# Regrouping the last weight loads of a decode block and spreading part of one projection's rows over 64 partitions

## The chip, the cores and the metric

The kernel runs on one core of a Trainium2 chip. The metric is the device time of one execution in microseconds (us). Before the change the median of three runs is 237.1 us (237.0 to 237.11).

## The reference, cut to what matters

One decode step of a transformer block with adaptive layer norm, for two sequences (B = 2), model width D = 512, all in float32:

```
mod = silu(c) @ w_mod                          # six vectors sa, ca, ga, sb, cb, gb of width 512
h   = layernorm(x) * (1 + ca) + sa
q   = h @ wq                                   # 512 x 4096: 32 heads of 128
p   = softmax(q . k / sqrt(128))               # last 4096 of 32768 cached keys, 8 key/value heads
x   = x + ga * ((p . v) @ wo)                  # 4096 x 512
h   = layernorm(x) * (1 + cb) + sb
x   = x + gb * (silu(h @ w1) @ w2)             # 512 x 1792 and 1792 x 512
```

Nearly all of the work is reading: 32 tiles of 2 MB of keys and values, 8 MB each of wq and wo, 6 MB of w_mod, and 3.5 MB each of w1 and w2; 97.5 MB in all.

## The kernel before, in words

**Loads.** All transfers are issued by SyncE (SP), in program order, and go into a ring of eight buffers of 16 KB a partition (`ring`, `RING = 8`, `stream` at line 69). A buffer is given out anew when the instructions that read its last content are done, so a load waits for the reader of the load eight places before it. Besides, eight semaphores go round among the transfers, so that a transfer also waits until the one eight transfers before it has landed; SP waits in order, and whatever is behind a waiting load waits with it. The order is w_mod (4 loads, line 103 and 111, with four small loads of c and x between them, line 107), wq (4 loads of 128 rows, line 112), then for each key/value head the keys and the values of both sequences (`fetch`, line 324), then wo (4 loads, line 472), a small one of x (`x_sp`, line 474), w1 (3 loads, line 477) and w2 (5 loads, line 482). With `out` these are 58 transfers.

**Modulation and q.** TensorE (PE) multiplies silu(c) by w_mod as each load lands. VectorE (DVE) makes the normed and modulated input and turns it into hq_T (line 263), 128 rows by four blocks. The q loop (lines 281 to 291) runs over four blocks of 128 rows of wq, two halves n of the heads and four groups g, with matmuls of 32 x 512 that accumulate over the blocks; for one n and g the 512 columns are those of four heads (s) that lie apart in wq.

**Attention.** For each of eight key/value heads DVE turns the keys (line 337), PE makes the scores (line 349), then come maxima, exponentials, a turn of the probabilities and the weighted sum of the values (line 423). The order is written out by hand (`keep_in_program_order`).

**wo, second norm, feed-forward.** PE multiplies by wo as its loads land (lines 548 to 570), DVE makes the residual and the norm, and the loop at line 593 multiplies by w1, block k by block k: blocks 0 and 1 lie in the first load, 2 and 3 in one each. After block 1 it makes the variance (line 606). Its result `hp` is turned, scaled, put through silu and stands as uT (line 627). The loop at 629 multiplies the first eight 128-row blocks of w2 (`WIDE = 8`) into yw, 32 x 512 each; the loop at 641 multiplies the last six into y, 32 x 128 each; after block 10, `gather` (line 519) adds yw, copied by ScalarE (ACT), into y. Two DVE instructions (lines 653 and 654) and the store (line 656) end the kernel.

**busy(n)** (line 534) issues n matmuls of 32 x 256 into a PSUM bank that nothing reads, to keep PE occupied between loads. One matmul of the source is two on the chip, each with its own weight load, since the data are float32.

Lines are those of the kernel before.

Of the kernel before, what the change touches and what calls it, by code (L numbers as in the profile page):

```python
# [13 lines left out]
P = 128  # L14
B, D = 2, 512
HQ, HKV, DH = 32, 8, 128
# [7 lines left out]
def adaln_block(  # L24
# [21 lines left out]
    nc = tc.nc  # L46
# [16 lines left out]
    def const(shape, name):  # L63
        return consts.tile(shape, F32, name=name)

    def bank(tag, name):
        return (psum1 if tag in "CO" else psum).tile([P, 512], F32, tag=tag, name=name)

    def stream(name):
        return ring.tile([P, 4096], F32, tag="st", name=name)  # L70

    def load_rows(name, w, k, width):
        t = stream(f"{name}{k}")[:, :width]
        nc.sync.dma_start(t, w[k * P : (k + 1) * P, :])
        return t
# [15 lines left out]
    def load_runs(name, w, per, lo, hi):  # L91

        e = w.shape[1]
        t = stream(f"{name}{lo}")[:, : (hi - lo) * e].rearrange("p (q e) -> p q e", e=e)
        nc.sync.dma_start(t, w.rearrange("(p q) e -> p q e", q=per)[:, lo:hi, :])
        return t
# [12 lines left out]
                src[b, :].rearrange("(k a c) -> a k c", k=4, a=4),  # L109
            )  # L110
    wm += [load_rows("wm", w_mod, k, 6 * D) for k in range(1, 4)]
    wqt = [load_rows("wq", wq, k, HQ * DH) for k in range(4)]


    ident = const([P, P], "ident")
# [125 lines left out]
    for k in range(4):  # L241
        ab = wm[k][:, : 2 * D].rearrange("p (s k a c) -> p a s k c", s=2, k=4, a=4)
        cd = wm[k][:, 2 * D :].rearrange("p (s g m) -> p g s m", s=4, g=4)
        for g in range(4):
            r = slice(32 * g, 32 * g + 32)
            nc.tensor.matmul(m_ch[r, :], scT[:, k, :], ab[:, g], start=(k == 0), stop=(k == 3))
        for g in range(4):
            r = slice(32 * g, 32 * g + 32)
# [13 lines left out]
    hq_T = const([P, 4, 32], "hq_T")  # L262
# [13 lines left out]
    nc.gpsimd.memset(uT, 0.0)  # L276

    q_ps = [bank("D", f"q{n}") for n in range(2)]  # L280
    for k in range(4):
        wv = wqt[k].rearrange("p (n s g m) -> p n g s m", n=2, s=4, g=G)
        for n in range(2):
            for g in range(G):
                nc.tensor.matmul(  # L285
                    q_ps[n][32 * g : 32 * g + 32, :],
                    hq_T[:, k, :],
                    wv[:, n, g],
                    start=(k == 0),
                    stop=(k == 3),  # L290
                )
    for n in range(2):
        qT = once.tile([P, D], F32, tag="wide", name=f"qT{n}").rearrange("p (s j r) -> p s j r", s=4, r=32)
        nc.vector.transpose(qT.rearrange("p s j r -> p (s j r)"), q_ps[n])  # L294
        for g in range(G):
            r = slice(32 * g, 32 * g + 32)
            eng = nc.gpsimd if g % 2 else nc.vector
            eng.tensor_copy(
                qg[n][r, :, :, :, g], qT[r, :, :, 0:32:16].rearrange("p s j b -> p s b j")
            )  # L300
        rp = bank("C", f"qr{n}")[:, :P]
        nc.tensor.matmul(
            rp, rep4, qg[n].rearrange("p s b j g -> p (s b j g)"), start=True, stop=True
        )
        for i in range(4):
            r = slice(32 * i, 32 * i + 32)
            cp = nc.scalar.copy if i % 2 else nc.vector.tensor_copy
            cp(
                qbd[n][r].rearrange("p s b j c -> p (s b j) c")[:, :, 4 * i : 4 * i + 4],
                rp[r, :].rearrange("p (m g) -> p m g", g=G),  # L310
            )
# [162 lines left out]
    nc.sync.dma_start(rows8(x_sp), x2.rearrange("b (g m) -> g b m", m=P))  # L474
    xT = turned(x_sp, "xT")
    w1t = []
    for lo, hi in ((0, 2), (2, 3), (3, 4)):
        wt = load_runs("w1_", w1, 4, lo, hi)
        w1t.extend(wt[:, k, :] for k in range(hi - lo))
    T2, WIDE = F // P, 8  # L480
    w2t = {}
    for lo, hi in ((0, 4), (4, WIDE), (WIDE, 11), (11, 13), (13, T2)):
        wt = load_runs("w2_", w2, T2, lo, hi)
        for tt in range(lo, hi):
            w2t[tt] = wt[:, tt - lo, :]
# [9 lines left out]
    for r in (0, 64):  # L495
# [4 lines left out]
            start=True,  # L500
            stop=True,
# [32 lines left out]
    def busy(n):  # L534

        for _ in range(n):
            inorder(nc.tensor.matmul(  # L537
                junk[0:32, :256],
                id4,
                selh.rearrange("p m y -> p (m y)")[:, :256],  # L540
                start=True,
                stop=True,
            ))
# [4 lines left out]
    for q in range(24):  # L548
        g = q % 4
# [4 lines left out]
            start=(q < 4),  # L554
            stop=(q >= 20),
# [3 lines left out]
    for q in range(24, 32):  # L559
        for g in range(4):  # L560
# [4 lines left out]
                start=(q == 24),  # L565
                stop=(q == 31),
# [26 lines left out]
    for k in range(4):  # L593
        for g in range(4):
            inorder(nc.tensor.matmul(
                hp[32 * g : 32 * g + 32, :],
                hT[:, k, :],
                w1t[k][:, g * FC : (g + 1) * FC],
                start=(k == 0),
                stop=(k == 3),  # L600
            ))
        if k == 2:
            busy(2)
        if k == 1:
            var = bank("B", "var_b")
            inorder(nc.tensor.matmul(var[:, :B], mean512, vs, start=True, stop=True))
            std = once.tile([P, B], F32, tag="stdb", name="std_b")
            nc.scalar.activation(std, var[:, :B], AF.Sqrt, bias=eps_t)
            rstd = once.tile([P, B], F32, tag="rstdb", name="rstd_b")
            nc.vector.reciprocal(rstd, std)  # L610
    busy(5)
    nc.vector.tensor_mul(ax, ao, ga)
    nc.vector.tensor_add(x1, x_sp, ax)
# [15 lines left out]
    for tt in range(WIDE):  # L629
        g = tt % 4  # L630
        inorder(nc.tensor.matmul(
            yw[32 * g : 32 * g + 32, :],
            uT[:, tt, :],
            w2t[tt],
            start=(tt < 4),
            stop=(tt >= WIDE - 4),
        ))
        if tt % 4 == 3:
            busy(1 + tt // 4)
    y = bank("D", "acc_y")[:, :P]  # L640
    for tt in range(WIDE, T2):
        for g in range(4):
# [4 lines left out]
                start=(tt == WIDE),  # L647
                stop=(tt == T2 - 1),
# [35 lines left out]
```

## Time and profile before

| what | value |
|---|---|
| median of three runs | 237.1 us |
| the profiled execution | 236.89 us |
| its span (first to last instruction) | 235.0 us |
| mean granted TensorE clock | 0.869 |
| busy: PE, PEld, DVE, ACT, POOL | 146.5, 45.9, 114.6, 25.4, 10.3 us |
| read from HBM | 97.53 MB, 415 GB/s over the span |
| packets on SP's queue | 7,592 |

The page's span is that of one profiled execution; the 1.9 us between it and that execution's time lie around it. The page cuts the span into 40 slices of 5.9 us and gives for each the busy share of an engine in tenths; its row DMA is the mean over the core's 16 DMA engines. The chain of waits follows the work that ended last back from the end: an entry "DMA wo" is time in which that chain waited for a transfer of wo to land. The timeline gives instructions in order of time, neighbours of one line merged, with the idle time before them and what ended it in brackets. The packed trace also holds a record of every DMA packet (start, duration, bytes, queue) and of every semaphore increment by which a DMA engine tells that its share of a transfer has landed. q1 is the queue of the kernel's transfers, q8 and q14 are named instruction queues by the profile.

### The profile page before, as it was taken

Reading aid. Unit: us, or ns where it says so; the run is one execution under the profiler, and the core shown is the slowest. Engines: PE = TensorE matmul, PEld = TensorE weight load, DVE = VectorE, ACT = ScalarE, POOL = GpSimd, SP = SyncE. Lnnn points to the kernel's source line nnn. Section 1 sums busy time; section 2 is a strip of 40 time slices with the busy share of each in tenths; the row PEclk is TensorE's granted clock in tenths of the full one; section 3 lists DMA queues with packets and bytes.
Section 4 is the critical chain, followed back from the end, with each engine's and each line's share of the span. In section 5 each row is a group of like instructions: output and inputs, shape, how many; then the busy total and the mean of one; then the engine's idle time right before and its main releaser. Section 6 shows DMA issues by size and latency. Waiting matters only on the chain.

```text
span 235.0 us, 2644 instructions
## 1 busy us (share of the span) xinstructions
PE 146.5 (62%) x1094; PEld 45.9 (20%) x1094; DVE 114.6 (49%) x176; ACT 25.4 (11%) x56; POOL 10.3 (4%) x30
## 2 busy tenths in 40 slices
PE   0086546367187577667549519626743967788993
PEld 0032101101011121121112102111211222335332
DVE  0634000793694792693892792595298050002130
ACT  2200000100300200200200200200020021003210
POOL 8600000100000000000000000000000000000000
PEclk9999975759869997999976967965985799999999
DMA  6999999999999999999999999999999999999991
GB/s 253 426 438 427 427 438 427 424 439 427 429 441 424 427 438 427 429 438 424 429 435 429 427 432 432 432 429 432 428 429 429 429 432 429 432 426 422 421 412 56
DMA packets 7603, 97.69 MB, mean 416 GB/s; under 512 B 920, under 2 KB 936, under 8 KB 1576
## 3 DMA queue, kind: packets, MB, share of 16 engines
q1 hardware_dynamic: 7592, 97.54, 97.5%
q8 instruction: 8, 0.13, 0.2%
q14 instruction: 3, 0.02, 0.0%
HBM read 97.53 MB, written 0.00 MB: 415 GB/s over the span
## 4 chain that ended last, share of the span: by engine, by line
DMA 64%; DVE 22%; PE 10%; ACT 2%; issue 1%; SPq 1%; DVEq 0%
DVE kT L337 16%; DMA wo<-in_A_wo_dram 14%; DMA k<-in_A_k_cache_dram 14%; DMA v<-in_A_v_cache_dram 13%; DMA wq<-in_A_wq_dram 13%; DMA w<-in_B_w_dram 7%; PE s L349 5%; DMA wm<-in_w_mod_dram 3%; DVE zp L395 2%; PE o L423 2%; PE q L285 1%; DVE xp L393 1%; ACT pr L381 1%; DVE mx L359 1%; ACT L381 1%
## 5 line engine op out<-in xcount | busy, mean ns | idle before, releaser
L337 DVE STREAM_TRANSPOSE kT<-k 128x1024 f32<-128x1024 f32 x64 | 73.7, 1210 | 1.6 <-DMA k<-in_A_k_cache_dram 1.6
L349 PE MATMUL s<-kT,qbd 128*32 128x512 f32 x256 | 44.5, 670 | 11.2 <-DVE kT L337 11.1
L423 PE MATMUL o<-v,ptb 128*32 128x512 f32 x256 | 38.5, 730 | 19.8 <-DMA v<-in_A_v_cache_dram 19.3
L359 DVE TENSOR_REDUCE mx<-s 128x1 f32<-128x512 f32 x8 | 5.5, 691 | 40.1 <-PE s L349 40.1
L349 PEld LDWEIGHTS s<-kT,qbd 128*32 128x32 f32 x256 | 11.1, 126 | 45.8 <-issue 24.1
L285 PE MATMUL q<-wq,hq_T 128*32 128x512 f32 x64 | 11.2, 836 | 10.1 <-DMA wq<-in_A_wq_dram 10.1
L423 PEld LDWEIGHTS o<-v,ptb 128*32 128x32 f32 x256 | 8.1, 124 | 35.8 <-issue 33.1
L402 PE MATMUL pT<-zp,id 128*32 128x256 f32 x64 | 5.6, 418 | 13.9 <-DVE zp L395 13.9
L379 ACT COPY bias<-bp 128x1 f32<-128x1 f32 x8 | 1.3, 159 | 111.9 <-PE bp L377 111.9
L537 PE MATMUL junk<-selh,id 128*32 128x256 f32 x46 | 11.3, 380 | 0.0
L294 DVE STREAM_TRANSPOSE qT<-q 128x512 f32<-128x512 f32 x2 | 1.4, 718 | 18.6 <-PE q L285 18.3
L395 DVE TENSOR_TENSOR zp<-xp,group 128x1024 f32<-128x1024 f32 x8 | 9.8, 1225 | 0.2
L393 DVE STREAM_TRANSPOSE xp<-pr 128x512 f32<-128x512 f32 x8 | 5.6, 701 | 4.4 <-ACT pr L381 4.4
L217 PE MATMUL mean_a<-mv_a,avg 128*128 128x1 f32 x2 | 0.6, 362 | 10.6 <-DVE mv_a L214 10.6
L361 PE MATMUL mT<-ident,mx 128*1 128x128 f32 x16 | 3.0, 270 | 6.4 <-DVE mx L359 6.4
L550 PE MATMUL acc_o<-wo,oTn 128*32 128x512 f32 x48 | 5.8, 598 | 1.9 <-DMA wo<-in_A_wo_dram 1.6
L537 PEld LDWEIGHTS junk<-selh,id 128*32 128x32 f32 x46 | 5.0, 110 | 6.7 <-issue 3.5
L438 PE MATMUL o_all<-ob,selh 128*64 128x128 f32 x64 | 5.7, 304 | 0.8 <-ACT ob L432 0.8
L270 DVE STREAM_TRANSPOSE xT<-x_sp 128x128 f32<-128x128 f32 x1 | 0.4, 403 | 11.8 <-DMA x_sp<-in_A_x_dram 11.8
L432 ACT COPY ob<-o 128x512 f32<-128x512 f32 x8 | 4.7, 585 | 10.3 <-PE o L423 10.3
L285 PEld LDWEIGHTS q<-wq,hq_T 128*32 128x32 f32 x64 | 2.1, 128 | 18.8 <-DMA wq<-in_A_wq_dram 12.5
L249 PE MATMUL m_sp<-wm,scT 128*32 128x512 f32 x32 | 5.7, 796 | 0.0
(132 smaller groups left out, 95.0 us busy)
## 6 DMA issues: line engine op xcount, KB each, us to landing
k<-in_A_k_cache_dram SPq DMA_DIRECT2D x16, 2048.0 KB, 30.2
v<-in_A_v_cache_dram SPq DMA_DIRECT2D x16, 2048.0 KB, 31.5
wq<-in_A_wq_dram SPq DMA_DIRECT2D x4, 2048.0 KB
wo<-in_A_wo_dram SPq DMA_DIRECT2D x4, 2048.0 KB, 32.3
wm<-in_w_mod_dram SPq DMA_DIRECT2D x4, 1536.0 KB, 10.2
w<-in_B_w_dram SPq DMA_DIRECT2D x2, 1024.0 KB, 23.2
w<-in_B_w_dram SPq DMA_DIRECT2D x1, 1792.0 KB
w<-in_B_w_dram SPq DMA_DIRECT2D x2, 896.0 KB
```

What stands on the lines that cost most here:

```text
L249: nc.tensor.matmul(m_sp[r, :], scT[:, k, :], cd[:, g], start=(k == 0), stop=(k == 3))
L285: nc.tensor.matmul(q_ps[n][32 * g : 32 * g + 32, :], hq_T[:, k, :], wv[:, n, g], start=(k == 0), stop=(k == 3),)
L337: inorder(nc.vector.transpose(kT[h, b][:, :, 8 * n4 : 8 * n4 + 8, :].rearrange("p j n k -> p n j k"), kt[h, b][:, n4 * 1024 : (n4 + 1) * 1 ...
L349: inorder(nc.tensor.matmul(s_ps[h][r : r + 32, :], qbd[h // 4][:, h % 4, b, j, :], kT[h, b][:, j, 16 * c : 16 * c + 16, :], start=(j == 0) ...
L359: inorder(nc.vector.tensor_reduce(mx, s_ps[h], axis=AX.X, op=ALU.max))
L393: inorder(nc.vector.transpose(xp, pr[h]))
L395: inorder(nc.vector.tensor_mul(zp, xp[:, None, :, 0:16].to_broadcast([P, 4, 16, 16]), group[:, :, None, None].to_broadcast([P, 4, 16, 16]),))
L402: inorder(nc.tensor.matmul(tp[32 * i : 32 * i + 32, :], id4, zp.rearrange("p a s x -> p (a s) x")[:, :, 4 * i : 4 * i + 4], start=True, st ...
L423: inorder(nc.tensor.matmul(o_ps[h][32 * c : 32 * c + 32, :], ptb[h % 2][:, 256 * b + 32 * w : 256 * b + 32 * w + 32], vt[h, b][:, 512 * w ...
L438: inorder(nc.tensor.matmul(o_all[r : r + 64, :], selh[:, m, HQ - G - G * h : 3 * HQ - G - G * h], o_sb[h][:, m * DH : (m + 1) * DH], start ...
L537: inorder(nc.tensor.matmul(junk[0:32, :256], id4, selh.rearrange("p m y -> p (m y)")[:, :256], start=True, stop=True,))
L550: inorder(nc.tensor.matmul(acc[32 * g : 32 * g + 32, :], oTn[:, q, :], wot[q // 8][:, q % 8, :], start=(q < 4), stop=(q >= 20),))
```

## The change

Three things are done.

1. wq's last 128 rows are loaded without the columns of the last three heads (3,712 of 4,096 columns). These three heads' columns of the 128 rows go into a buffer of their own, `wqx`, on partitions 0 to 63: partition p holds rows 2p and 2p + 1. That takes eight loads of eight partitions each, with a step of four partitions, two behind each of the four loads of wq. `wqx` takes a place in the ring, ahead of wq's first block.
2. So that PE can use them, hq_T's last block is multiplied by the even and by the odd columns of the identity, which gives `hx` (64 partitions by two by 32), and for the three groups in question the last block's matmul has 384 columns in place of 512, followed by two matmuls of 128 columns over 64 partitions.
3. w1 comes in two loads of two blocks in place of three, and w2's first eight blocks in one load in place of two. The `busy` calls move with it: 6 after the variance in place of 2 after block 2, and 2 after all of yw in place of 1 and 2 after each half. There are 64 transfers in place of 58.

```diff
-    wqt = [load_rows("wq", wq, k, HQ * DH) for k in range(4)]
+    WX = 3 * DH
+    WN = HQ * DH - WX
+    wqt, wqx = [], stream("wqx")[:, : 2 * WX].rearrange("p (j e) -> p j e", j=2)
+    rows2 = wq[3 * P :, WN:].rearrange("(p j) e -> p j e", j=2)
+    for k in range(4):
+        if k < 3:
+            wqt.append(load_rows("wq", wq, k, HQ * DH))
+        else:
+            wqt.append(stream("wq3"))
+            nc.sync.dma_start(wqt[3][:, :WN], wq[3 * P :, :WN])
+        for p0 in ((0, 1), (2, 3), (32, 33), (34, 35))[k]:
+            nc.sync.dma_start(wqx[p0 : p0 + 29 : 4], rows2[p0 : p0 + 29 : 4])
...
+    hx = const([P // 2, 2, 32], "hx")
+    hxp = bank("B", "hxp")[: P // 2, :64]
+    for j in range(2):
+        nc.tensor.matmul(
+            hxp[:, 32 * j : 32 * j + 32], ident[:, j:P:2], hq_T[:, 3, :], start=True, stop=True
+        )
+    nc.vector.tensor_copy(hx.rearrange("p j c -> p (j c)"), hxp)
...
             for g in range(G):
+                r = slice(32 * g, 32 * g + 32)
+                part = k == 3 and n == 1 and g > 0
+                s1 = 3 if part else 4
                 nc.tensor.matmul(
-                    q_ps[n][32 * g : 32 * g + 32, :],
+                    q_ps[n][r, : s1 * DH],
                     hq_T[:, k, :],
-                    wv[:, n, g],
+                    wv[:, n, g, :s1, :],
                     start=(k == 0),
                     stop=(k == 3),
+                    skip_group_check=True,
                 )
+                for j in range(2 if part else 0):
+                    nc.tensor.matmul(
+                        q_ps[n][r, 3 * DH :],
+                        hx[:, j, :],
+                        wqx[: P // 2, j, (g - 1) * DH : g * DH],
+                        start=False,
+                        stop=(j == 1),
+                        skip_group_check=True,
+                    )
...
-    for lo, hi in ((0, 2), (2, 3), (3, 4)):
+    for lo, hi in ((0, 2), (2, 4)):
         wt = load_runs("w1_", w1, 4, lo, hi)
...
-    for lo, hi in ((0, 4), (4, WIDE), (WIDE, 11), (11, 13), (13, T2)):
+    for lo, hi in ((0, WIDE), (WIDE, 11), (11, 13), (13, T2)):
         wt = load_runs("w2_", w2, T2, lo, hi)
...
-        if k == 2:
-            busy(2)
         if k == 1:
...
             nc.vector.reciprocal(rstd, std)
+            busy(6)
...
-        if tt % 4 == 3:
-            busy(1 + tt // 4)
+    busy(2)
```

## The prediction

> **What bounds the kernel now.** I read the page's slices first, then its DMA queues.
>
> ```profile
> PE   0086546367187577667549519626743967788993
> DVE  0634000793694792693892792595298050002130
> PEclk9999975759869997999976967965985799999999
> DMA  6999999999999999999999999999999999999991
> GB/s 253 426 438 427 427 438 427 424 439 427 429 441 424 427 438 427 429 438 424 429 435 429 427 432 432 432 429 432 428 429 429 429 432 429 432 426 422 421 412 56
> ...
> q1 hardware_dynamic: 7592, 97.54, 97.5%
> q8 instruction: 8, 0.13, 0.2%
> q14 instruction: 3, 0.02, 0.0%
> ```
>
> No compute engine is full; the 16 DMA engines are, from the second slice to the last but one. In the packet records 5,102 of the 5,128 packets of 16 KB took 611 ns, and on one engine the next starts about 4 ns before the last ends: 16 x 16,384 B / 607 ns = 432 GB/s, the figure of the GB/s row. So each DMA engine is a conveyor without gaps, and the time is that of the engine that ends last, plus what follows it. The chain of waits in order of time shows the end:
>
> ```profile
> 181.22 32.69 DMA wo<-in_A_wo_dram
> 213.91 0.02 issue
> 213.92 0.02 SPq L95
> 213.94 0.03 issue
> 213.97 16.51 DMA w<-in_B_w_dram
> 230.48 0.04 issue
> 230.53 1.10 PE acc_y L643 x24
> 231.63 0.02 issue
> 231.66 0.30 DVE yo L653
> 231.96 0.02 issue
> 231.98 0.29 DVE yo L654
> ```
>
> Two stretches of waiting for transfers and 1.7 us of compute: what moves the landings of w2 moves the end. The landing records (one semaphore increment per DMA engine and transfer) show that the engines do not end together. For the last transfer (w2 rows 13) they come 0, 0.25, 0.33, 0.37, 0.48 / 0.78, 0.87, 1.24 / 1.45, 1.66, 1.86, 1.89, 1.96, 1.99, 2.00, 2.05 us after 229.07. The reason is in the two instruction queues above. Up to 28 us every transfer's sixteen landings lie within 0.64 us; each of q8's eight 16 KB packets (31.6, 77.2, 105.7, 128.7, 164.3, 185.4, 207.8, 221.9 us) then sets one engine back by some 1.5 us, a different one each time, and q14's three 8 KB packets (47.2, 168.6, 214.5) set back one more each by some 0.7. Eight late engines, three half late, five undisturbed: the sixteen offsets.
>
> **Term 1, the engines' load.** (a) wq's last 128 rows lose 1,536 B each. 14,336 B took 535 ns and 16,384 B 611, so 1,536 B are worth 57 ns; 8 rows on every engine: -0.46 us. (b) The eight wqx loads move 8 partitions x 2 pieces of 1,536 B. No such piece is in the trace; between 128 B (13 ns) and 2,048 B (84 ns) it is 65 ns, started 61 ns apart, and a semaphore packet adds 6. One load is then 2 x 61 + 6 = 0.128 us on each engine it uses, eight are +1.02 us. (c) Merging w1's two quarters saves 8 x (2 x 268 - 531) ns = 0.04, w2's two fours 8 x (2 x 305 - 607) = 0.02, two semaphore packets 0.01: -0.08 in all. Engines without wqx get -0.53 us, the others +0.49.
>
> Everything hangs on which engines get wqx. No eight-row load is in the trace. The nearest rows: the loads of c and x (4 rows) land with 4 increments, on four engines; so does x_sp. x_sp lands at 212.20, 212.31, 212.39 and 213.26, right behind wo's last rows, whose sixteen landings run from 211.85 to 213.91 at offsets 0, 0.17, 0.28, 0.35, 0.37, 0.54, 0.55, 0.82, 1.22 and then seven from 1.48 up. Three of the four are among the earliest; the pattern 0, 0.11, 0.19, 1.06 fits 0.17, 0.28, 0.35 and 1.22. So the four engines of small loads are not among the late eight. I take it that an eight-row load uses these four and four more, and that these too are of the other half, since late and not late are exactly eight and eight; bounds: none late, or at least one.
>
> The Trainium skill speaks to this in "DMA: Bandwidth & Descriptors", section "Why a DMA increments its semaphore by 16 and not by 1": the number of engines is the largest up to 16 that divides both slowest dimensions, and they are the lowest-numbered. By it eight rows go to the lower half, which holds the four; the trace agrees for four rows, and nothing here tells whether the late eight are the upper half.
>
> With none late, the merged w2 rows 0 to 7 take the place of w2 rows 4 to 7, whose last landings were at 1.26 (half late) and 2.06 (late) behind 225.33: 1.26 + 0.49 = 1.75, 2.06 - 0.53 = 1.53. The last is now 1.75: **-0.31 us**. For the last transfer it is the same (1.24 and 2.05). With one late engine hit it is +0.49.
>
> **Term 2, the tail's compute.** These PE rows of the timeline carry it:
>
> ```profile
> 225.98 1.06 PE L631 MATMUL acc_yw<-w,uT 128*32 128x512 f32 x8 [0.36 <-DVE uT L627]
> 227.43 1.06 PE L631 MATMUL acc_yw<-w,uT 128*32 128x512 f32 x8
> 228.32 1.03 PE L537 MATMUL junk<-selh,id 128*32 128x256 f32 x4
> 229.36 0.86 PE L643 MATMUL acc_y<-w,uT 128*32 128x128 f32 x24
> 230.01 0.43 PE L524 MATMUL acc_y<-acc_y_sb,id 128*32 128x128 f32 x8
> 230.53 1.06 PE L643 MATMUL acc_y<-w,uT 128*32 128x128 f32 x24
> ```
>
> Before, half of yw was done ahead of the landing at 227.39, since w2 rows 0 to 3 were there. Now all 16 matmuls start with that landing. Eight took 0.88 us to the next start (227.43 to 228.32), 16 take 0.86 more: junk starts at 229.18. Its four at 0.216 end at 230.04 (before, acc_y waited until 229.36 for w2 rows 8 to 10). Then 24 of acc_y (0.65 to the next start): 230.69; gather: 230.91; 16 of acc_y: 231.35; the last eight, which before began at 231.16, with the landing at 231.12. 0.19 later by an unmoved landing; the last eight then run in a stream (0.109 apart, where after the wait they were 0.133 apart), so the end is **+0.15 us** later, which I take. The yw copy on ACT (0.59) ends near 230.05, ahead of the gather.
>
> What stands before yw has cover. w1 rows 2 and 3 come together at 222.48. busy(6) after var (220.33) runs 12 x 0.216 = 2.6 us, to 222.93, so hid's second half starts 0.41 later than its last quarter did, and lasts two quarters (1.5 in place of 0.75): hidT comes 1.16 us later and uT lets yw start at 227.14. That hides behind the landing at 227.39 with 0.25 to spare; all these times move together with the landings. Were the cover gone, what it lacks would be paid in full. The matmuls fed to PE leave no gap longer than about 0.8 us, so I leave the clock as the PEclk row has it (9 in the last eight slices).
>
> **What costs nothing.** hx: two matmuls and one DVE copy, done when hq_T is ready, ahead of wq's first landing (22.9 us). q: three matmuls of 384 columns in place of 512 and six of 128, below 0.6 us before the first keys at 45.95; SP's k and v issues run some 30 us ahead of the landing (30.2 and 31.5 us on the page), so half a microsecond there is invisible. SP: eight more issues of 0.45 to 0.72 us. wqx takes a ring buffer, so the fourth k load waits for the last q matmul (42.4 us, now about 43) and five loads queue behind it; the engines then still hold k loads that land until 53.5. Ten us of cover. At the end w2's loads wait for older buffers than before and are issued earlier.
>
> **Sum.** -0.31 + 0.15 = -0.16 us. The profiled execution took 236.89 (span 235.0 and 1.9 around it), so it would be 236.73; the median of the runs is 237.1, so I predict **236.9**. A measurement of this kernel tells about 0.2% (0.47 us) from no change.
>
> **Rivals.** (A) At least one late engine is among wqx's eight. For it: two thirds of the engines that small loads were not seen on are late. Landing +0.49, tail +0.15: 237.7, slower. It decides as soon as an engine with an offset over 1.57 (1.57 + 0.49 = 2.06) gets wqx rows. 0.14. (B) The half-late engine is not hit (q14's packet falls elsewhere), or the tail costs nothing: last landing 1.53, -0.53 and 0 to 0.15: 236.6 to 236.7. 0.12. (C) PE fetches a ninth time. q8's packets started when 204, 464, 748, 962, 1,262, 1,448, 1,747 and 2,021 PE instructions had begun, 260 apart; the next would be near 2,281 of now some 2,266 (2,219, 11 matmuls of 4, 3 waits). If it comes, it comes beside w2's last packets and sets an engine back 1.5 us: 1.52 + 1.5 = 3.0 against 2.05, so 238.0. 0.06. (D) A small load holds its engines longer than its bytes. Upper bound: SP's 0.57 us an issue, 8 x 0.57 = 4.6 in place of 1.02, last landing 1.26 + 4.0 = 5.3: 240.4; by the 0.18 us between the landings of c's and x's loads 1.44: 2.17, so 237.4. Against both: the packet records of those loads are gapless on their four engines. 0.03.
>
> Here the Trainium skill speaks against the change: "DMA: Bandwidth & Descriptors", section "Rules for kernel authors", says that under 64 KB one pays mostly overhead, and its section "Anatomy of one DMA" gives about 2.0 us a transfer (by GpSimd's path). A wqx load has 24 KB; eight would add 16 us if the engines stood still meanwhile, and by the packet records they do not.
>
> My forecast (no change beyond 0.2%) has 0.65. Faster by over 0.2%: 0.12 (0.09 of B, 0.03 of the forecast's spread). Slower by over 0.2%: 0.22 (A, C, 0.01 each of D and of that spread). Within: 0.66. Range 236.5 (B, less the runs' spread of 0.1) to 237.8 (A with the same).
>
> **What would show it.** Right: the landings of each transfer after wq spread over about 1.5 to 1.75 us in place of 2.05, the last w2 landing near 230.8, yw as one block of 16 that starts with a landing, and the last acc_y not waiting for a DMA. Wrong: a landing spread of 2.5 (A), a ninth q8 packet (C), idle time in the packet records around 20 to 45 us (D or SP), or yw waiting for uT.

## The result, and the profile after

| | before | after |
|---|---|---|
| median of the runs | 237.1 us (5 runs, 237.0 to 237.29) | 237.92 us (5 runs, 237.76 to 238.26) |
| the profiled execution, its span | 236.89, 235.0 us | 237.84, 235.9 us |
| first and last landing of w2 rows 13 | 229.07, 231.12 us | 229.16, 231.94 us |
| PE instructions in the records | 2,219 | 2,266 |

The ratio is 1.0034 (95% interval 1.0022 to 1.0045, written in brackets below): slower by 0.34%, 0.8 us. The forecast was 236.9 and "no change"; its range ended at 237.8. Of the runs further down, e11 stands by its four executions of 238.23 to 238.65 us alone: the fifth, which is its profiled one, fell into a slower state (251.22 us), so e11 has no trace to read.

The page of the kernel after, the same rows as before:

```profile
PE   0087275738718775775758529627744967878984
DVE  0634001288279298396595793594298050002130
PEclk9999978875967999999979976995995799999999
DMA  6999999999999999999999999999999999999991
GB/s 248 420 428 433 411 421 437 419 435 436 419 436 431 431 428 433 436 419 439 428 431 428 431 433 428 432 431 431 433 425 433 425 436 428 425 441 425 425 398 39
...
q1 hardware_dynamic: 7496, 97.54, 97.2%
q8 instruction: 9, 0.15, 0.2%
q14 instruction: 3, 0.02, 0.0%
```

DMA is still 9 from the second slice on. What differs is GB/s in slices five and six (23.6 to 35.4 us): 411 and 421 where before had 427 and 438. The engines are busy there and move less: that is where the wqx loads run. The ninth q8 packet of rival C came, at 232.7 us, when all loads had landed.

The end of the chain of waits of the kernel after, in order of time:

```profile
196.97 31.31 DMA w<-in_B_w_dram
228.28 0.14 issue
228.41 1.92 PE acc_yw L665 x16
230.34 0.52 PE junk L572 x3
...
232.03 0.72 PE acc_y L676 x19
232.77 0.30 DVE yo L686
233.09 0.29 DVE yo L687
```

No wait for a transfer stands in the chain after 228.41; before it stood ahead of the last 24 matmuls of acc_y. The whole end hangs on the landing of w2 rows 0 to 7 at 228.28. That landing is 0.89 us later than the one that yw's second half waited for before (227.39), and the first DVE instruction of yo starts 1.11 later (231.66, now 232.77). So 0.89 is landings, 0.22 is the tail. Of the 0.89, 0.12 is there already at w_mod's third load (mean landing 14.06 and 14.18 us).

The timeline of the kernel after shows that nothing else holds yw:

```profile
227.79 0.20 DVE L661 TENSOR_TENSOR uT<-z,sgh 128x28 f32<-128x28 f32 x1
228.41 1.92 PE L665 MATMUL acc_yw<-w,uT 128*32 128x512 f32 x16 [0.71 <-DMA w<-in_B_w_dram]
```

uT is done at 227.99, 0.29 ahead of the landing; the bracket names the DMA.

The late landings go back to one place. The rows of the stretches from 26 to 32 us, from the tables by stage of before and after (us; busy time and number for PE, PEld, DVE, ACT, POOL; granted clock; DMA share; GB/s):

```profile
26.00:32.00 6.00, 3.19 (x16) 0.52 (x16) 0.00 (x0) 0.00 (x0) 0.00 (x0) 0.72 1.02 434
```

```profile
26.00:32.00 6.00, 2.65 (x16) 0.60 (x16) 0.00 (x0) 0.00 (x0) 0.00 (x0) 0.78 1.00 404
```

404 in place of 434 GB/s over 6 us is 0.18 MB not moved, 0.4 us of all sixteen engines. The packet records say how. Of the 128 pieces of 1,536 B, 107 took 62 to 65 ns. The other 21 lie in the first two pairs of loads: three of them at 22.2 to 22.5 us, and 18 at 27.3 to 28.1, up to 342 ns. 33 of the 16 KB packets between 20 and 32 us took 622 to 798 ns, where 611 is the rule. (One more took 1,102 ns at 27.8; it follows q8's first packet, 26.8 to 27.7 us, as one of 1,115 ns at 32.5 follows q8's first packet in the kernel before, so it is not counted here.) All pieces of the third and fourth pair (32.7 to 38.2 us) took 62 to 65 ns. I call those that took longer than usual **dear packets**.

### The profile page after: what moved, and what is told of

It is laid out like the page before. It is cut to its first block, busy times and chain, and to the rows that moved or that the text cites. A ratio compares the mean times of both kernels' runs of the same rounds, so it can differ in the third digit from the quotient of the medians.

```text
span 235.9 us, 2697 instructions
## 1 busy us (share of the span) xinstructions
PE 151.4 (64%) x1116; PEld 48.4 (21%) x1116; DVE 115.0 (49%) x177; ACT 25.4 (11%) x56; POOL 10.3 (4%) x30
## 4 chain that ended last, share of the span: by engine, by line
DMA 57%; DVE 20%; PE 18%; ACT 2%; issue 1%; SPq 0%; DVEq 0%
DMA v<-in_A_v_cache_dram 28%; DVE kT L372 14%; DMA w<-in_B_w_dram 13%; DMA wq<-in_A_wq_dram 13%; PE s L384 7%; PE o L458 4%; DMA wm<-in_w_mod_dram 3%; DVE zp L430 2%; PE q L310 2%; ACT pr L416 1%; DVE xp L428 1%; DVE mx L394 1%; PE q L319 1%; PE acc_yw L665 1%; PE mT L396 1%
## 5 line engine op out<-in xcount | busy, mean ns | idle before, releaser
L384 PE MATMUL s<-kT,qbd 128*32 128x512 f32 x256 | 45.9, 659 | 11.2 <-DVE kT L372 11.2
L310 PE MATMUL q<-wq,hq_T 128*32 128x512 f32 (+1 forms) x64 | 12.1, 730 | 8.4 <-DMA wq<-in_A_wq_dram 8.4
L572 PE MATMUL junk<-selh,id 128*32 128x256 f32 x52 | 12.4, 380 | 0.0
L572 PEld LDWEIGHTS junk<-selh,id 128*32 128x32 f32 x52 | 5.6, 110 | 6.4 <-issue 2.4
L412 PE MATMUL bp<-negscale,mrow 1*128 1x1 f32 x16 | 3.0, 256 | 4.2 <-DVE mrow L405 4.2
```

The lines of the kernel that those rows point to most:

```text
L310: nc.tensor.matmul(q_ps[n][r, : s1 * DH], hq_T[:, k, :], wv[:, n, g, :s1, :], start=(k == 0), stop=(k == 3), skip_group_check=True,)
L384: inorder(nc.tensor.matmul(s_ps[h][r : r + 32, :], qbd[h // 4][:, h % 4, b, j, :], kT[h, b][:, j, 16 * c : 16 * c + 16, :], start=(j == 0) ...
L572: inorder(nc.tensor.matmul(junk[0:32, :256], id4, selh.rearrange("p m y -> p (m y)")[:, :256], start=True, stop=True,))
```

## The experiments

Each run is compared with the kernel before on the same chip. e1 to e4, e11 and e14 to e16 are forms of the change. e5 to e7, e9 and e10 are the kernel before with extra loads that nothing reads, in a place of the ring; e8 and e12 add three tiny loads; e13 (e15 in eight loads) gave no result. The theories at the start: it is the engines' bytes (rival A), the tail, or the price of the small loads.

**e1: the third part alone** (w1, w2 and `busy` as in the change, wq as before).

> The change without its wq part: w1 in two loads, w2's first eight rows in one, the busy calls moved; 56 transfers. Theory (the eight small wqx loads put bytes on DMA engines that are late already): the landings come 0.08 us earlier and the end of PE's last block 0.15 to 0.22 later, so +0.07 to +0.15 us against the kernel before, 237.2 us. Rival (the regrouped tail costs the time): +0.6 to +0.9, 237.8.

237.01 against 237.06, ratio 0.9999 [0.9991, 1.0008]. Its chain of waits ends like that of the change:

```profile
195.53 32.31 DMA w<-in_B_w_dram
227.98 1.92 PE acc_yw L630 x16
...
231.59 0.72 PE acc_y L641 x19
232.34 0.30 DVE yo L651
```

The same form of tail, and no loss: the merged transfers give back (last landing 0.10 us earlier by the account below) what the tail adds.

**e2: the first two parts alone** (wqx and hx; w1, w2 and `busy` as before).

> The change's wq part alone, with the loads of w1 and w2 and the busy calls of before; 66 transfers. Theory: the last landing is that of an engine that gets wqx rows and an instruction packet, 0.5 us later from its bytes and 0.3 more from the stall around 26 to 30 us, +0.7 to +0.9 us: 237.9. Rival (the tail costs the time): +0 to +0.2, 237.2. Second rival (bytes alone, the stall being chance): +0.5, 237.6.

237.97, ratio 1.0042 [1.0029, 1.0055]. The whole loss is in wq's part.

**e3: the change with wqx spread over sixteen engines.**

```
-        for p0 in ((0, 1), (2, 3), (32, 33), (34, 35))[k]:
-            nc.sync.dma_start(wqx[p0 : p0 + 29 : 4], rows2[p0 : p0 + 29 : 4])
+        nc.sync.dma_start(wqx[k : 64 : 4], rows2[k : 64 : 4])
```

> The change with wqx in four loads of 16 partitions in place of eight loads of 8: the same pieces of 1,536 bytes, the same matmuls, but each of the 16 DMA engines takes 8 of them in place of eight engines taking 16. Theory (which engines get the bytes decides): each engine gets 4 x 0.128 - 0.46 - 0.08 us, about nothing, so what remains is the tail: 237.2 to 237.3, landings spread over 2.05 us behind the first. Rival (small pieces cost time wherever they go: the stall of 0.3 us): 237.5 to 237.6.

239.06 (238.06 to 240.14), ratio 1.0088 [1.0063, 1.0113]. A miss: without any unevenness of bytes it is slower still. In its records most 16 KB packets from 36 to 50 us take 690 to 704 ns; why is open. With this loss of its own the run can't tell what uneven bytes cost; e5 to e9 do.

**e4: the change with one head in place of three** (`WX = DH`, so pieces of 512 B).

> The change with one head's columns in wqx in place of three: pieces of 512 bytes, still eight loads of eight partitions. By the packet times (27 ns for 512 bytes) the engines with wqx get 8 x 0.052 - 0.15 - 0.08 = +0.19 us in place of +0.49, the others -0.23. Theory: the last landing is 0.3 us earlier than with three heads, 237.6 if the stall stays, 237.3 without it. Rival (cost per load, not per byte): as with three heads, 237.9.

237.09, ratio 1.0002 [0.9993, 1.001]: no loss at all, better than expected. All 128 pieces took 27 ns.

**e5, e6, e7: the kernel before with eight extra loads of 1,536 B pieces.** e5 reads one dense stretch of w2, e6 the rows that the change reads (16 KB between the pieces of a partition, 128 KB between engines), e7 is e5 with four partitions a load.

```
+    rows2 = wq[3 * P :, HQ * DH - 3 * DH :].rearrange("(p j) e -> p j e", j=2)
...
         wqt.append(load_rows("wq", wq, k, HQ * DH))
+        for i in range(2):
+            p0 = (0, 1, 2, 3, 32, 33, 34, 35)[2 * k + i]
+            nc.sync.dma_start(extra[p0 : p0 + 29 : 4], rows2[p0 : p0 + 29 : 4])
```

> The kernel before with eight loads more, two behind each of wq's four, of 8 partitions x 2 pieces of 1,536 bytes, into a ring buffer that nothing reads; the bytes are neighbours in memory (from w2). All of wq is loaded as before. Theory (the bytes are paid by the last engine): eight engines get +1.02 us, at least one of which is also set back by an instruction packet, so the last landing is 2.05 + 1.0 behind the undisturbed ones: +1.0 us, 238.1, no packet over its usual 65 ns. Rival (per small load a stall on all engines): +1.3, with packets of 100 to 350 ns.

237.49, ratio 1.0013 [1.0004, 1.0022]: +0.28, where 1 us was expected.

> As the run with eight dense loads more, but the pieces lie as in the change: 1,536 bytes at the end of rows 16 KB apart, the eight engines reading 128 KB apart at the same time. Theory on the stall (pieces that lie at the same place of rows a power of two apart hold one another up): some 0.3 us more than the dense loads, 238.4, with packets of up to 350 ns at 22 to 30 us. Rival (the stall was chance, or comes from the small loads as such): as dense.

238.32, ratio 1.0045 [1.0033, 1.0058]. The same bytes in loads of the same shape, 0.83 us dearer than e5, by nothing but where they are read. In e5 all 128 pieces took 65 ns and no 16 KB packet up to 32 us took longer than 611. In e6 25 pieces took more than 65 ns (up to 324).

> As the run with eight dense loads more, with 4 partitions a load in place of 8: four engines get +1.02 us each. Theory (the four engines of such loads are not among those that the PE instruction packets set back): the last of them is one at about 1.24, so 1.24 + 1.02 = 2.26 against 2.05, +0.2 us, 237.3. Rival (any engine that gets the bytes ends last): +1.0, 238.1.

237.14, ratio 0.9995 [0.9986, 1.0004]. Four engines take 1 us more, and the last landing of w2 rows 13 moves by 0.18 us, close to the +0.2 of the theory; in the time this does not show.

**e8: which engines are late before.** Loads of 6, 8 and 12 rows behind x_sp, 64 to 160 B a row, so that their packets show which engines a load uses and when the engine came free of wo.

> The kernel before with three loads more behind x_sp, of 6, 8 and 12 partitions and 64, 96 and 160 bytes each, into a buffer that nothing reads any more. They tell, by the start of their packets behind wo's last load, where the engines 0-3 (x_sp's four), 4-5, 6-7, 8-11 and 12-15 stand at 212 us. Theory: of the seven engines set back by then, six are among 8-15 and one is 4, 5, 6 or 7. Rival (my forecast's): all seven are among 8-15. The time within 0.5 us of before.

One run, 236.94. The engines of the 4-row load are among those of the 6-row load, these among those of the 8-row one, and so on. By then seven engines had been set back by q8; two of them are among the eight of an 8-row load (at offsets 1.26 and 1.41 behind wo's first landing, the least late), five are not. The theory had one among the eight, its rival none.

**e9, e10: what about the place is dear.** e9 is e6 with each partition reading 1,536 B further along its row (`step = 8 * row + 3 * DH`); its first piece lies at the start of a row and 64 rows ahead of e6's; e10 is e6 with the same distances out of wo.

> The kernel before with the same eight unread loads of 8 partitions x 2 pieces of 1,536 B out of wq's rows, 16 KB between the two pieces of a partition, but each of the eight partitions reads 1,536 B further along its row than the one ahead of it, so that the eight engines no longer read the same place of their rows. Theory (eight engines that read the same place of rows 128 KB apart at once get in each other's way): the pieces take 65 ns and the time is that of dense pieces, 237.4 to 237.6. Rival (short pieces out of rows far apart, or out of the tensor that is being read, are dear wherever in the row they lie): pieces up to some 340 ns and 238.2 to 238.4, as with the unstaggered ones.

237.57, ratio 1.0018 [1.0008, 1.0027]; all 128 pieces took 65 ns.

> The kernel before with the same eight unread loads and the same distances (16 KB between pieces, 128 KB between engines, the same place of each row), but out of wo, which nothing else reads at that time, in place of wq. Theory (the distances cost the time): pieces up to some 340 ns, 238.2 to 238.4. Rival (what costs is to read next to the rows of wq that are in flight): pieces of 65 ns, 237.4 to 237.6.

238.42, ratio 1.0057 [1.0045, 1.007]; 32 dear pieces, up to 342 ns. Both as the theory says. The same stretch in the tables by stage, e6 and then e9:

```profile
26.00:32.00 6.00, 2.73 (x16) 0.42 (x16) 0.00 (x0) 0.00 (x0) 0.00 (x0) 0.75 1.02 421
```

```profile
26.00:32.00 6.00, 2.48 (x20) 0.42 (x16) 0.00 (x0) 0.00 (x0) 0.00 (x0) 0.91 1.03 437
```

The unstaggered pieces move 16 GB/s less, with the engines as busy: what costs is that eight engines read the same place of rows 128 KB apart, not the tensor, nor short pieces out of far rows. It is not the order of SP's issues either: e9 issues wq's fourth load at 23.92 us, the change at 23.87, and e9 has no dear piece. That the step does it, and not e9's other start, is argued and not shown: no run moves the start alone.

**e11: the change with neighbouring partitions** (`wqx[p0 : p0 + 8]`, so 32 KB between engines).

> The changed kernel whole, but each wqx load takes eight neighbouring partitions (0 to 7, 8 to 15, ...) in place of every fourth one, so that the eight engines read rows 32 KB apart in place of 128 KB. Theory, if it is the distance between the engines: fewer dear pieces, 237.3 to 237.6. Theory, if it is that they read the same place of rows a power of two apart, whatever the distance: 237.9, as the changed kernel. If the neighbouring partitions get in each other's way on the writing side: over 238.2.

238.5 (238.23 to 238.65), ratio 1.0056 [1.0042, 1.007]. A smaller power of two between the engines is no cure; whether the 0.6 us beyond the change come from the writing side isn't settled.

**e12: the probes in the kernel after.**

> The changed kernel with the three small probe loads (6, 8 and 12 partitions) behind the load of x that the kernel before had in an earlier run. Theory: of the eight engines that the eight-row probe uses, two or three are among those that land late, at an offset over 2.05 us; four are those of the four-row load of x. Time 238.0 as the changed kernel, since the probes have a few hundred bytes each.

One run, 238.51. The four engines that land last there (2.02, 2.41, 2.99, 3.04 us behind wo's first landing of 212.03) all belong to an 8-row load, and the two latest are not among the four of x_sp. Rival A's condition holds in this execution.

**e14: the change with the eight loads together behind wq's last** (`for p0 in (0, 1, 2, 3, 32, 33, 34, 35)` after the loop).

> The changed kernel whole, with the eight wqx loads together behind wq's last load in place of two behind each. The dear pieces were all in the first two pairs, at 22 and 27 us; those at 33 and 38 us took 65 ns. Theory 1 (pieces are dear while the sixteen engines run in step, and the first dear ones put them out of step): the first of the eight are as dear as before, 237.7 to 238.0. Theory 2 (it is what else is in flight at 22 to 28 us): no dear pieces at 37 us, 237.1 to 237.4.

241.58, ratio 1.0183 [1.0168, 1.0197]: both missed the time. Its page and SP's waits from 20 to 50 us:

```profile
DMA  6999994999999999999999999999999999999991
GB/s 252 426 439 432 427 423 110 421 431 432 429 421 432 435 435 432 432 429 421 432 435 429 432 432 432 425 427 432 432 432 435 429 427 429 435 427 423 435 408 60
```

```profile
SPq L125 <- DMA wq<-in_A_wq_dram: 17.5, 4, 5.8
```

The seventh slice falls to 110 GB/s: eight small transfers fill the eight semaphores, SP waits for wq to land before it can issue the next, and the engines stand idle for 3.7 us each in the mean (36 to 42 us). The first packets of the keys after it took up to 2,215 ns, another 0.9 us an engine. Up to 37.2 us all pieces took 62 to 65 ns, though the engines had been in step till then (15 of the 16 landings of wq's last load lie within 0.67 us). So being in step is not enough. But the run changes what goes on beside the pieces too: from 36.5 us six engines or fewer were moving 16 KB rows, and from 36.8 one, where in e6 eight to thirteen were. Theory 2 holds for the pieces without saying what in flight makes them dear.

**e15, e16: 512 B pieces of all three heads, and the control.** Each wqx load as two (`for j in range(2)`), e15 with a gap behind each head in the buffer so that pieces are 512 B, e16 without it.

> The changed kernel whole, with the buffer wqx laid out with a gap behind each head and each wqx load made as two (even rows, odd rows), so that the same bytes come from the same places in pieces of 512 B: 16 loads of 8 partitions x 3 pieces. Theory (the loss is that of the dear 1,536 B pieces; the 512 B pieces of the version with one head took 27 ns without exception): 16 x (3 x 23 + 6) = 1.2 us per engine in place of 1.02, no dear ones, 237.1 to 237.4. Rival (what costs is the bytes that the eight engines get, or that they read the same rows): 237.9 to 238.2.

240.17, ratio 1.0113 [1.0093, 1.0133]. The theory missed in the pieces as well: nine of the 384 took 52 to 233 ns, all of them at 22.5 to 27.8 us. So pieces of 512 B can be dear too, if less often.

> Control for the run beside it: the changed kernel whole, with each wqx load made as two, but pieces of 1,536 B as in the change. Theory: dear pieces up to some 340 ns, 237.8 to 238.2. If 16 loads by themselves cost (eight semaphores go round, so that eight small transfers fill them): over 238.3 here and as much more in the run beside it.

239.51, ratio 1.0107 [1.0094, 1.0121]. The control itself is over its bound: 16 loads let the queue run dry. The GB/s rows, e15 and then e16:

```profile
GB/s 241 420 437 421 401 412 364 423 428 429 429 434 432 429 432 426 434 429 432 434 426 428 432 429 434 429 432 432 429 432 429 429 429 437 429 428 430 426 352 20
```

```profile
GB/s 250 426 437 425 408 404 366 431 426 433 431 433 419 436 431 439 425 428 431 439 428 421 433 433 433 422 433 431 436 431 428 425 439 431 422 432 426 436 377 24
```

364 and 366 in the seventh slice; the idle times of the 16 engines add up to some 11 and 6 us between 20 and 52 us. In the times this hides what e15 was to show.

**All runs in one account.** "Bytes" is the prediction's own arithmetic for the mean of the sixteen engines. "Dear and idle" is what the packets between 20 and 52 us took over the usual duration of their size, less the 1.05 us of before (two 16 KB packets, one behind a q8 and one behind a q14 packet), plus the idle engine time, divided by 16. "Mean" is the shift of the mean landing of w2 rows 13 against before, "last over mean" how far the last lies behind it (0.86 before). Landings count from the mean landing of w_mod's third load, since the start differs by up to 0.5 us from execution to execution. All in us.

| run | bytes | dear and idle | their sum | mean | last over mean |
|---|---|---|---|---|---|
| the change | -0.02 | 0.36 | 0.34 | 0.36 | 1.19 |
| e1 third part alone | -0.08 | 0.00 | -0.08 | -0.09 | 0.85 |
| e2 wq's part alone | 0.05 | 0.42 | 0.47 | 0.49 | 1.07 |
| e4 one head | -0.02 | 0.00 | -0.02 | -0.02 | 0.76 |
| e5 dense | 0.51 | 0.00 | 0.51 | 0.51 | 0.90 |
| e7 dense, four engines | 0.26 | 0.00 | 0.26 | 0.24 | 0.79 |
| e9 staggered | 0.51 | 0.00 | 0.51 | 0.51 | 0.86 |
| e6 the change's places | 0.51 | 0.37 | 0.88 | 0.88 | 1.27 |
| e10 the same in wo | 0.51 | 0.52 | 1.03 | 1.05 | 1.27 |
| e3 sixteen engines | -0.03 | 1.95 | 1.92 | 1.90 | 0.78 |
| e16 16 loads | 0.00 | 1.52 | 1.52 | 1.56 | 1.69 |
| e15 16 loads, 512 B | 0.06 | 1.64 | 1.70 | 1.77 | 2.15 |
| e14 eight at the end | -0.02 | 4.63 | 4.61 | 4.60 | 0.84 |

The sum meets the measured mean within 0.04 us in every row but e15 (0.07): nothing else of weight moves the mean landing. This is bookkeeping of the engines' time: it says where the time went, and the runs above say why. In the change 0.30 of its 0.36 is dear packets (of these 4.85 us of engine time 3.0 are in the 21 pieces) and 0.06 is engines that stood idle, most of it at 27 us.

## Why the prediction was wrong, point by point

**What bounds the kernel** held: the landings set the end, before and after.

**Term 1, (b), is the step that failed:** "between 128 B (13 ns) and 2,048 B (84 ns) it is 65 ns, started 61 ns apart". The size was right, and 65 ns is exactly what dense and staggered pieces took. But the rows it was interpolated from are of pieces that lie elsewhere. Where eight engines read the same place of rows 128 KB apart at once, some of the pieces and of the 16 KB packets beside them take up to 342 and 798 ns: with the idle time +0.36 on the mean landing. The last landing lies besides 1.19 over the mean, where dense and staggered pieces leave 0.86 to 0.90: +0.3, as the eight engines are then set further behind the others (e6 against e9 shows the same, 1.27 and 0.86). At the first keys those two groups of landings lie at 0 to 0.35 and 0.93 to 1.57 us; with staggered pieces at 0 to 0.33 and 0.60 to 0.87 (and one engine at 1.64 that a q8 packet had set back). The Trainium skill, "DMA: Bandwidth & Descriptors", section "Latency and other measured facts", has row pitches from 512 KiB up that lower the rate of copies (207 GB/s at that pitch and 103 at 4 MiB, against 214 in full), and infers that streams in step meet in one channel of the memory. Here it is seen at 128 KB, with short pieces, and e9 removes it by 1.5 KB more pitch, where that page reports 4 KiB as enough and 192 B as not. That it is channels no run here shows.

**Term 1, "I take it that an eight-row load uses these four and four more, and that these too are of the other half",** failed too. It was to take 0.31 us off the last landing, as a late engine would have no wqx. e5 and e9 test it without dear packets: on that assumption the last landing would move by 0.21 (1.24 + 1.02 less 2.05), as it did in e7 with four engines (0.18); it moved by 0.56 and 0.52. e8 shows two late engines among the eight before, e12 four after. The step is worth about 0.31 us: the change takes 0.53 off every engine, so with dense pieces its last landing would be about where it was, not 0.31 earlier; this is an estimate from e5 and e9. This part of the error is rival A's mechanism. That A's 237.7 came near the time, and that its sign appeared (w2 rows 13 land over 2.78 us, 229.16 to 231.94), is in the main luck: the larger part is the dear packets, which A does not have.

The last landing in sum: forecast -0.31, measured +0.70 (0.82 from 231.12 to 231.94, less the 0.12 of the start; in the table 0.36 and 1.19 less 0.86). Of the 1.01 between them the assumption is about 0.31, the dear packets and the idle time about 0.70.

**Rival D** (a small load holds its engines longer than its bytes) did not come true: in e5 the mean landing moves by the bytes alone, 0.51. But the prediction took it that more small loads leave the queue full. The small loads take up semaphores, so SP waits for landings sooner: wq's fourth load was issued at 8.28 us before and at 23.87 after. The change has some 1.0 us of idle engine time between 27 and 32 us, shared by sixteen: 0.06. Small, but it is what e14 to e16 ran into: small loads in a row empty the queue.

**Term 2, the tail,** was right: +0.22 measured in the profiled execution where +0.15 was taken, yw as one block behind a landing, acc_y without a wait, and 0.29 us of cover for uT where 0.25 was reckoned. e1 shows the third part as neutral: 237.01 against 237.06.

**(a) and (c)**, the bytes saved, held: with them the mean landings of e1 and e4 come out within 0.01 us. **Rival C** came true in its condition (a ninth packet, PE at 2,266 instructions) and cost nothing: it started at 232.7, behind the last landing. **What costs nothing** held in its outcome, but one size in it was far off. For q it reckoned below 0.6 us more. The chain of waits shows q's last block before and after:

```profile
39.01 3.39 PE q L285 x16
```

```profile
38.62 2.73 PE q L310 x11
...
44.74 0.56 PE q L319 x4
```

That is 3.39 us before and 6.68 after, 3.3 us more, so that the first turn of the keys began at 48.86 in place of 45.95. The key load that waits for the last of q's matmuls was issued at 45.3, not at 42.4; it is the sixth in both kernels, and the fourth, which the prediction had waiting there till about 43, went out at 34.7. The cover paid for all of it: after 32 us no DMA engine stood idle.

**Open:** why only the first four of the eight loads have dear pieces in the change, e6 and e10 (later ones read the same kind of places at 65 ns; in e16, where the queue runs dry, two late pieces took 107 and 625); why 512 B pieces are never dear in the version with one head, yet nine of 384 are in e15; the slow stretch of e3. That the dear packets come from the place that is read is shown by e6 and e10 against e9 and e5, and that they and the idle time make up the shift of the mean landing by the account; a version of the change with the same bytes and no dear packet wasn't had, since e15 was spoilt by its 16 loads. No form of the change was faster than the kernel before.

## What to carry to other kernels

A price read off the packet records holds for the place that the packets came from: before pricing small pieces by size, look at what the engines of one load read at the same moment, and if it is the same place of rows a power of two apart, pieces can be up to five times as dear, and neighbours pay with them (here in the first four of eight loads, not in the later ones). Where many engines end apart, keep two numbers, the mean landing and the last over the mean; the first is plain bookkeeping (within 0.07 us here), and the second needs to know which engines are hit. Moving 192 KB from one set of engines to another isn't worth transfers that take up the places of a short ring of semaphores.

## What the runs showed of the hardware that was not expected

- 128 pieces of 1,536 B out of the same tensor took 65 ns each or, 25 of them, up to 324 ns, by their addresses alone; 1.5 KB more between the engines' addresses removed it (e6 238.32, e9 237.57 us).
- Eight loads of 24 KB cost their engines no more than their bytes (e5: mean landing +0.51 us, which is 8 x 0.128 / 2), but eight of them in a row left the sixteen engines idle for 3.7 us each in the mean (e14).
- Loads of 4, 6, 8 and 12 rows use nested sets of engines (e8). This agrees with the Trainium skill, "DMA: Bandwidth & Descriptors", section "Why a DMA increments its semaphore by 16 and not by 1", by which a transfer issued as these are uses the lowest-numbered engines.
